# Half the FFN's columns at a time, most of the last group's V kept on chip, and early gradient steps staged in halves

## The chip, the cores and the metric

The kernel runs on one core of a Trainium2 chip. The metric is the device time of one execution in microseconds. A profile of one execution is read beside it.

## What is computed

The reference is a small transformer block for a single token, forward and backward (`jax.vjp`). All tensors are bf16.

```python
def _A_ref(x, k_cache, v_cache, wq, wo):      # D = 448, 16 heads of Dh = 256 over 8 groups
    W = min(4096, max(256, Sk // 4))          # Sk = 32768, so the window is W = 4096
    q = (x @ wq)...
    k = repeat(k_cache[:, :, Sk - W:, :], 2); v = repeat(v_cache[:, :, Sk - W:, :], 2)
    p = softmax(q . k * Dh ** -0.5); o = p . v
    return o.reshape(...) @ wo

def _B_ref(x, w_gate, w_up, w_down):          # F = 1792
    return ((x @ w_gate) * (x @ w_up)) @ w_down

h  = x + _A_ref(layernorm(x), k_cache, v_cache, wq, wo)
h2 = h + _B_ref(layernorm(h), w_gate, w_up, w_down)
# outputs: h2, and the gradients of x, k_cache, v_cache, wq, wo, w_gate, w_up, w_down
```

The gradients of the two caches have the caches' full size, 8 x 32768 x 256 each. They are zero outside the last 4096 positions of each group, and these zeros have to be written as well: 16 regions of 14.68 MB, 235 MB in all.

## The kernel before

**Layout.** Most data lives in `BIG`, one SBUF tile of 128 partitions. It is cut into nine slots of 8192 bf16 columns (`SLOT`, 32 positions of 256), and a tail behind them. A slot holds one group's K or V window: partition p has 32 consecutive positions, 16 KB in one piece. V of group g lies in slot g; K moves through slots 3 to 8 (`K_SLOT`); V of group 7 takes slot 7, after K of group 6.

**Three queues of DMA.** SP issues the fills (`FILL`): each writes one region of zeros from 16 rows of the tile `zeros`, in rows of 8192 (`ZW`) or 14336 columns (`NW`). `next_fills(n)` issues the next n of the list `regions`, and `deal_fill` at the end deals the last region to the DMA engines in uneven parts. POOL (`IO`) issues all loads of windows and weights (`io_load`, in order), the stores of the weight gradients and of `out_2`; `deal_some` sends a few fills there. ACT issues the stores of `out_3`. The scheduler of the framework keeps each engine's order; `in_order` adds an order without a wait. DMAs of SP and ACT take eight completion counters in turn, and a DMA that takes a counter again waits until the one that had it before has landed.

**Forward.** For each group, `moments(g)` (L405) forms the weighted sums over K and V, and issues the next group's scores and softmax. In the last group it also issues the load of wo's first 9 blocks (L435).

**Middle.** After the groups, wo (32 blocks of 448 columns), w_gate, w_up and pieces of w_down are loaded into slot 7, slot 8 and the tail (`A0`, `WU0`, `WG0`, `WD0`, L442 to L446), over V and K of group 7. Fourteen blocks of wo that lie where w_up goes are copied to PSUM first (`park`, L513), since they are needed again. Then come: the product with wo (`ao`, L524), layernorm, the products with all columns of w_gate and w_up (L538), w_down in four pieces (`CH`, `load_wd`, `down_grad` L542, `y` L566), the broadcast of the two gradient rows over the partitions (L578 to L590, into `bc2`), the products with w_gate and w_up (L593), the layernorm's backward pass, and the products with wo (L604). Both rows stay in `bc2` as sources for `out_6` and `out_7`.

**Backward loop.** For each group s = 0 to 7 (L777) 32 outer products are made on PE (`d_ps`, L784), and evicted by ACT and DVE in turn (`evac`, L305 and L307) into a pair of slots (`PAIR`), one for `out_2` and one for `out_3`. At the end of the step both are stored (L814). During a step the products of the next group's V (`dP`) are made, and DVE forms the weight gradients of `during` in pieces (`outer`, L653, with the store at L656). V of group 7, which the weights have overwritten, is loaded again in step 3 (L808). The order in which places become free is what ties a step to the stores of earlier ones:

```python
PAIR = [KS, 0, KS, 0, KS, 0, 5, KS]     # KS = 7
tail = eng.dma_start(out=o[0, g, Sk - W:, :]..., in_=pair[:, w])
```

Of the kernel before, what the change touches and what calls it, by code (L numbers as in the profile page):

```python
# [35 lines left out]
KS = 7  # L36
TAIL = 9 * SLOT
RING = TAIL + 6016
# [5 lines left out]
def kernel(  # L44
# [106 lines left out]
    Vw = [slot_kv(g) for g in range(G - 1)] + [Kw[G - 2]]  # L151
# [253 lines left out]
    def moments(g):  # L405
# [4 lines left out]
        for c in range(T // 2):  # L410
# [31 lines left out]
    A0 = KS * SLOT  # L442
    PARK = range(4, 18)
    WU0 = A0 + PARK[0] * D
    WG0 = A0 + 32 * D
    WD0 = WG0 + NI * HF  # L446
    CH = ((0, 0, 4), (0, 4, NI), (1, 0, 4), (1, 4, NI))
    assert WD0 + 4 * D == RING

    def wo_at(b):  # L450
        return A0 + b * D

# [7 lines left out]
    wg_sb = BIG[:, WG0:WD0]  # L460
    wu_sb = BIG[:, WU0:WU0 + NI * HF]
    wd_sb = BIG[:, WD0:RING].rearrange("p (m n) -> p m n", n=D)
# [4 lines left out]
    bc2 = [BIG[:, o:o + F].rearrange("p (i c) -> p i c", i=2) for o in (WD0, WD0 - F)]  # L467
# [21 lines left out]
    load_wo(9, 32)  # L489
    io_load(wg_sb, flat_rows(B_w_gate))  # L490
# [22 lines left out]
    def park(b):  # L513
        n = (b - PARK[0]) // 2
        w = tps.tile([128, D], u32, tag=f"w{n}", name=f"w{n}")
# [4 lines left out]
    for b in PARK[:-2:2]:  # L520
        park(b)
    ao = tps.tile([1, D], f32, tag="w6", name="ao")
# [4 lines left out]
    hX = const.tile([128, NI], f32)  # L527
    V_.tensor_tensor(out=hX[:], in0=rows_to_half(ao[:])[:], in1=xX[:], op=ALU.add)
    park(PARK[-2])
    io_load(wu_sb[:, 6 * HF:], flat_rows(B_w_up)[:, 6 * HF:])  # L530
    rstd2, xh2, xf2, xx2 = layernorm(hX[:], "ln2")

    gu_ps = ps.tile([128, 2, 2, NI], f32, tag="tmp", bufs=1, name="gu_ps")
    for w, w_sb in ((0, wg_sb), (1, wu_sb)):
        wv = w_sb.rearrange("p (i c) -> p i c", i=NI)
        for m in range(NI):
            for i in range(NI):
                P_.matmul(gu_ps[:, w, :, m], lhsT=wv[:, i, m::NI], rhs=xx2[:, i, :], start=(i == 0), stop=(i == NI - 1))  # L538
# [6 lines left out]
    down_grad(*CH[0])  # L545
    gu = const.tile([128, 2, FC], f32)
    V_.tensor_copy(out=gu[:], in_=gu_ps[:].rearrange("p w s m -> p w (s m)"))

    hh = const.tile([128, FC], f32)
    V_.tensor_tensor(out=hh[:], in0=gu[:, 0, :], in1=gu[:, 1, :], op=ALU.mult)  # L550
    hh_bf = const.tile([128, FC], bf16)
    V_.tensor_copy(out=hh_bf[:], in_=hh[:])

    y = ps.tile([1, D], f32, tag="tmp", bufs=1, name="y")
    hX2 = small.tile([128, NI], f32, tag="hX2", bufs=1)
    V_.tensor_scalar(out=hX2[:], in0=hX[:], scalar1=0.5, scalar2=None, op0=ALU.mult)
    for n, (s, m0, m1) in enumerate(CH):
        if n:
            load_wd(s, m0, m1)
            if n == len(CH) - 1:  # L560
                with tc.issue_after(queued[0].ins):
                    deal_some()
            down_grad(s, m0, m1)
        for m in range(m0, m1):
            c = NI * s + m
            P_.matmul(y[:], lhsT=hh_bf[:, c:c + 1], rhs=wd_sb[:, m - m0, :], start=(c == 0), stop=False, skip_group_check=True)  # L566
# [5 lines left out]
    dgu = const.tile([128, 2, FC], bf16)  # L572
    for w in range(2):
        V_.tensor_tensor(out=dgu[:, w, 0:FC], in0=d_hh[:], in1=gu[:, 1 - w, :], op=ALU.mult)

# [4 lines left out]

    P2 = const.tile([128, 2, NI], f32)
    for w, w_sb, ev in ((0, wg_sb, evac), (1, wu_sb, on_act)):
        for h in range(4):
            r = small.tile([2, HF // 4], bf16, tag="R", name="r")
            t = ps.tile([2, NI, 32], f32, tag="tmp", bufs=1, name="t")
            to_rows(r[:].rearrange("s (j m) -> s m j", m=NI), t[:], [dgu[:, w, m::NI] for m in range(NI)], 32 * h, ev)
            for i2 in range(2):
                bc = ps.tile([128, HF // 4], f32, tag="tmp", bufs=1, name="bc")
                P_.matmul(bc[:], lhsT=Par[:, i2:i2 + 128], rhs=r[:], start=True, stop=True)
                ev(bc2[w][:, i2, h * HF // 4:(h + 1) * HF // 4], bc[:])  # L590
        wv = w_sb.rearrange("p (i c) -> p i c", i=NI)
        for i in reversed(range(NI)):
            V_.tensor_tensor_reduce(out=wv[:, i, :], in0=wv[:, i, :], in1=bc2[w][:, i % 2, :], scale=1.0, scalar=0.0,  # L593
                                    op0=ALU.mult, op1=ALU.add, accum_out=P2[:, w, i:i + 1])
# [8 lines left out]
    for b in range(32):  # L603
        V_.tensor_tensor_reduce(out=wg_sb[:, 0:D], in0=parked.get(b, wo_b(b)), in1=dh_bc[:], scale=1.0, scalar=0.0,  # L604
                                op0=ALU.mult, op1=ALU.add, accum_out=doW[:, b:b + 1])
# [7 lines left out]
    od = small.tile([128, 32], f32, tag="ex", bufs=1)  # L613
# [24 lines left out]
    for b1 in range(0, 16, 4):  # L638
        r = wg_sb[0:2, b1 * 128:b1 * 128 + 512]
# [27 lines left out]
    def wq_product(w, i2, n):  # L667
        V_.tensor_tensor_reduce(out=slot(4)[:, SLOT - HQ:SLOT], in0=w, in1=dq_bc[:, i2, :], scale=1.0, scalar=0.0,  # L668
                                op0=ALU.mult, op1=ALU.add, accum_out=Pq[:, n:n + 1])

    def dxn():
        for h in range(2):
            wq_product(odd[:, h * HQ:(h + 1) * HQ], 0, NI + h)
            yield
# [4 lines left out]
    def dx_out():  # L679
# [12 lines left out]
        dx = slot(4)[0:1, SLOT - D:SLOT]  # L692
# [10 lines left out]
    def o67_job(buf, w, i0, i1):  # L703
        return outer(buf, (o6, o7)[w][:, i0:i1, :], i0, i1, lambda i: bc2[w][:, i % 2, :], xf2, HF)

    def o8_job(buf, b):
# [12 lines left out]
    begin = {3: 4, 5: 8, 6: 8}  # L719
    for job in (o67_job(half(KS + 1, 1), 1, 0, 4), o67_job(half(KS, 1), 1, 4, 7)):  # L720
        for _ in job:
            pass
# [22 lines left out]
    def factors(s):  # L745
        R_ps = ps.tile([128, 2 * Dh], f32, tag="tmp", bufs=1)
        for k, (E, rr) in enumerate(((Ed, do_rows), (Eq, q_rows))):
            ex = small.tile([H, 32, 4], bf16, tag="ex")
# [21 lines left out]

    for q in range(8):
# [5 lines left out]
    for s, g in enumerate(SEQ):  # L777
        R = Rb[:, s % 2, :]
        pair = BIG[:, PAIR[s] * SLOT:(PAIR[s] + 2) * SLOT].rearrange("p (w t d) -> p w t d", w=2, d=Dh)
        work = (None for job in during.get(s, ()) for _ in job)  # L780
        for t in range(T):
# [3 lines left out]
                      start=True, stop=True)  # L785
            if stored is None:
                evac(pair[:, :, t, :], d_ps[:])
            else:
                with tc.issue_after(stored.ins):
                    evac(pair[:, :, t, :], d_ps[:])  # L790
# [3 lines left out]
            if s + 1 < G:  # L794
# [18 lines left out]
        for w, o, eng in ((0, out_3, S_), (1, out_2, IO)):  # L813
            tail = eng.dma_start(out=o[0, g, Sk - W:, :].rearrange("(p t) d -> p t d", t=T), in_=pair[:, w])  # L814
            if eng is S_:
                in_order(tail, filled[0])
                stored = tail
# [36 lines left out]
```

## Time and profile before

| What | Value |
|---|---|
| median of 3 runs | 776.44 us (776.29 to 776.56) |
| the profiled execution: its time, its span | 776.47 us, 774.7 us |
| busy: PE, weight loads, DVE, ACT, POOL | 61%, 34%, 49%, 25%, 4% |
| moved | 330.09 MB: 48.33 read, 280.59 written |
| DMA packets | 19233 |
| first and last DMA of the w_down pieces issued | 269.8 and 333.9 us |
| last stores of the backward loop issued | 702.7 and 703.1 us |

The page cuts the span into 40 slices of 19.4 us and gives the share of busy time in each. Its line for the DMA is the mean over 16 DMA engines. The chain of work that ended last goes back from the last instruction to what released each step. Views by stretch give the busy time of each engine between two points of the span.

### The profile page before, as it was taken

The page shows a single profiled execution, that of the slowest core. Times are in us where ns is not written, and L with a number is a line of the kernel's source. Part 1 is how long each engine was busy: PE and PEld are TensorE (multiplying, and loading weights), DVE is VectorE, ACT ScalarE, POOL GpSimd, SP SyncE. Part 2 cuts the span into 40 slices and gives each one's busy share as a digit, 9 for nine tenths or more (in the row PEclk, how much of TensorE's full clock was granted, in tenths as well). Part 3 has the DMA queues.
Part 4 walks back from the last instruction along what each step waited for, and adds up shares of the span by engine and source line. Part 5 has one row for each costly group of instructions (what it writes and reads, how often), then busy time and mean ns, then how long its engine had stood idle before and what let it go on. Part 6 is the DMA issues. An engine that isn't in the chain of part 4 may idle for free. (4 is left out here: it accounts for less than half of the span.)

```text
span 774.7 us, 10961 instructions
## 1 busy us (share of the span) xinstructions
PE 471.5 (61%) x4427; PEld 263.5 (34%) x4472; DVE 377.3 (49%) x1141; ACT 190.5 (25%) x306; POOL 32.5 (4%) x70
## 2 busy tenths in 40 slices
PE   3889999999996323023315899895786865352000
PEld 2755665556553113011213534332232322120000
DVE  4166566655664112025576465764565545982000
ACT  0422443334220000003102444342242432121000
POOL 3000000000000000010001000000000000000000
PEclk9999999999998665555555555555555555555555
DMA  9999999999999999999999999999999999999998
GB/s 360 429 428 427 428 428 428 427 426 429 428 428 428 430 431 439 427 435 432 429 433 428 429 432 427 435 431 428 430 430 434 430 434 427 432 428 434 433 430 343
DMA packets 19233, 330.09 MB, mean 426 GB/s; under 512 B 1570, under 2 KB 1578, under 8 KB 2847
## 3 DMA queue, kind: packets, MB, share of 16 engines
q1 hardware_dynamic: 10953, 233.91, 70.4%
q0 software_dynamic: 6992, 78.24, 23.9%
q10 hardware_dynamic: 1238, 17.24, 5.2%
q8 instruction: 35, 0.57, 0.3%
q14 instruction: 15, 0.12, 0.0%
HBM read 48.33 MB, written 280.59 MB: 425 GB/s over the span
## 5 line engine op out<-in xcount | busy, mean ns | idle before, releaser
L415 DVE TENSOR_SCALAR BIG<-BIG,pf 128x256 bf16<-128x256 bf16 x512 | 114.7, 282 | 58.8 <-PE MT L419 26.4
L419 PE MATMUL MT<-BIG 128*128 128x512 bf16 x467 | 139.3, 400 | 5.1 <-DMA BIG<-in_A_v_cache_dram 4.3
L784 PE MATMUL d_ps<-BIG 32*128 32x512 bf16 x256 | 118.1, 602 | 39.8 <-DVE BIG L307 17.6
L305 ACT CAST BIG<-d_ps 128x512 bf16<-128x512 f32 x156 | 88.0, 589 | 136.9 <-PE d_ps L784 105.5
L360 PE MATMUL tr<-ident_bf,BIG 128*128 128x128 bf16 x1024 | 119.0, 268 | 4.0 <-DMA BIG<-in_A_k_cache_dram 3.0
L360 PEld LDWEIGHTS <-BIG 128*128 128x128 bf16 x1024 | 79.9, 119 | 40.0 <-issue 35.2
L311 ACT COPY BIG<-tr 128x1024 bf16<-128x1024 bf16 x64 | 64.6, 1012 | 108.9 <-PE tr L360 104.8
L307 DVE CAST BIG<-d_ps 128x512 bf16<-128x512 f32 x100 | 68.5, 687 | 26.2 <-PE d_ps L784 15.6
L422 PEld LDWEIGHTS <-BIG 128*128 128x128 bf16 x512 | 44.8, 99 | 52.0 <-issue 11.7
L307 DVE COPY BIG<-tr 128x1024 bf16<-128x1024 bf16 x60 | 41.4, 690 | 38.7 <-PE tr L360 38.7
L365 PEld LDWEIGHTS <-BIG 128*128 128x128 bf16 x1024 | 38.1, 103 | 62.3 <-DVE BIG L307 42.4
L422 PE MATMUL acc<-pT_all,BIG 128*128 128x2 bf16 x512 | 45.2, 165 | 9.1 <-DVE kbar L439 6.1
L419 PEld LDWEIGHTS <-BIG 128*128 128x128 bf16 x512 | 39.6, 100 | 22.7 <-issue 9.2
L425 PE MATMUL acc<-pT_all,BIG 128*128 128x2 bf16 x512 | 44.2, 164 | 0.0
L784 PEld LDWEIGHTS <-BIG 32*128 32x128 bf16 x256 | 21.2, 113 | 58.8 <-issue 34.9
L365 PE MATMUL dp<-doT,BIG 128*128 128x2 bf16 x512 | 24.3, 169 | 18.6 <-DVE BIG L307 17.5
L542 DVE CUSTOM_DVE_ANT_0 dh_bc<-BIG,dh_bc 128x448 bf16<-128x448 bf16 x14 | 8.7, 624 | 50.9 <-DMA BIG<-in_B_w_down_dram 50.7
L425 PEld LDWEIGHTS <-BIG 128*128 128x128 bf16 x512 | 30.0, 96 | 0.9
L566 PE MATMUL y<-BIG,hh_bf 128*1 128x448 bf16 x14 | 5.9, 565 | 35.9 <-DMA BIG<-in_B_w_down_dram 35.2
L365 PE MATMUL sT<-qT,BIG 128*128 128x2 bf16 x512 | 22.6, 165 | 1.1 <-ACT BIG L311 1.0
L244 PE MATMUL t<-one,xe 1*128 1x1 f32 x42 | 10.8, 323 | 13.1 <-DVE xe L243 13.1
L763 DVE TENSOR_TENSOR BIG<-r_ps,mrow 96x1024 bf16<-96x1024 bf16 (+2 forms) x15 | 18.3, 1223 | 0.8 <-PE r_ps L768 0.4
(192 smaller groups left out, 349.6 us busy)
## 6 DMA issues: line engine op xcount, KB each, us to landing
out_dram<-zeros SPq DMA_DIRECT2D x14, 14336.0 KB, 154.8
out_dram<-BIG POOLq DMA_DIRECT2D x9, 2048.0 KB, 39.3
BIG<-in_A_v_cache_dram POOLq DMA_DIRECT2D x8, 2048.0 KB, 25.8
out_dram<-BIG ACTq DMA_DIRECT2D x8, 2048.0 KB, 22.9
BIG<-in_A_k_cache_dram POOLq DMA_DIRECT2D x6, 2048.0 KB, 43.7
out_dram<-zeros SPq DMA_DIRECT2D x1, 11264.0 KB
out_dram<-zeros SPq DMA_DIRECT2D x1, 7680.0 KB, 61.5
out_dram<-zeros POOLq DMA_DIRECT2D x1, 4224.0 KB, 43.2
```

Of the source, the lines that this page charges most:

```text
L244: P_.matmul(t[:, i:i + 1], lhsT=c, rhs=one[0:1, 0:1], start=True, stop=True)
L305: S_.copy(out=out, in_=in_)
L307: last_copy[0] = V_.tensor_copy(out=out, in_=in_)
L311: S_.copy(out=out, in_=in_)
L360: P_.transpose(tr[:, i, dh, :], x_at(g, 4 * q + i)[:, dh * 128:(dh + 1) * 128], ident_bf[:])
L365: P_.matmul(out_ps[:, 4 * q + i, :], lhsT=xt[:, i, dh, :], rhs=vecT[:, 4 * g + dh:4 * g + dh + 3:2], start=(dh == 0), stop=(dh == 1))
L415: V_.tensor_scalar(out=pk[:, i, h, :], in0=K[:, t, :], scalar1=pf[:, t, h:h + 1], scalar2=None, op0=ALU.mult)
L419: P_.matmul(MT[hf][:], lhsT=v_at(g, t)[:, hf * 128:(hf + 1) * 128], rhs=pk[:, i, :, :].rearrange("p h d -> p (h d)"), start=(t == 0), stop ...
L422: P_.matmul(acc[:, 2 * hf:2 * hf + 2], lhsT=v_at(g, t)[:, hf * 128:(hf + 1) * 128], rhs=pT_all[:, g, t, :], start=(t == 0 and hf == 0), st ...
L425: mm = P_.matmul(acc[:, 4 + dk:7 + dk:2], lhsT=K[:, t, dk * 128:(dk + 1) * 128], rhs=pT_all[:, g, t, :], start=False, stop=(t == T - 1), s ...
L763: V_.tensor_tensor(out=rows[p0:p1], in0=r_ps[p0:p1, :].unsqueeze(1).to_broadcast([p1 - p0, 8, 128]), in1=mrow[p0:p1, :].unsqueeze(2).to_br ...
L784: mm = P_.matmul(d_ps[:].rearrange("p w d -> p (w d)"), lhsT=rows[32 * k:32 * k + 32, a, :], rhs=R[32 * k:32 * k + 32, :], start=True, sto ...
```

## The change

- w_gate and w_up are loaded and used in two halves of 896 columns (`load_wgu`), into the place of wo's first 14 blocks (now in slot 8), which are all copied to PSUM first. A half of w_gate is loaded by ACT in two DMAs, a half of w_up by POOL in two; a row is 1792 B. Gate and up rows are interleaved over partitions, so that one product of DVE covers both.
- wo, gate and up now lie in slot 8 and the tail. In slot 7 only the first 8 positions of V of group 7 are overwritten (`side`: pieces of w_down, the broadcast rows, scratch). These 8 are loaded again, ahead of the loop; the other 24 stay.
- wo comes in three pieces (9, 5 and 18 blocks). `y` is formed as columns (`yc`, `ycol`) and turned at the end.
- The rows for `out_6` and `out_7` are made a second time in the loop (`o67_job`).
- Steps 0 to 2 stage and store their pairs in two halves of 16 positions (`HALVES`), the others in slots two apart (`PAIR`). `out_8` moves from step 6 to ahead of the loop, `out_6` and `out_7` into steps 3 and 4, `out_5` to steps 5 and 6, `out_4` to steps 5 and 6.
- Of the fills, six, one and four are issued in the middle's places, not eleven at the start; fills 5 and 6 have rows of 8192 columns.

```diff
-KS = 7
+KS = 8
+KEPT = 14
+GONE = 8
...
-            f = NW if i >= 5 else ZW
+            f = NW if i >= 7 else ZW
...
-        next_fills(11)
+        next_fills(6)
...
-    Vw = [slot_kv(g) for g in range(G - 1)] + [Kw[G - 2]]
+    Vw = [slot_kv(g) for g in range(G)]
...
+            if c == 13 and g == G - 1:
+                load_wo(9, KEPT)
...
+    wgu_sb = BIG[:, wo_at(0):wo_at(KEPT)].rearrange("p (i c) -> p i c", i=NI)
+    side = BIG[:, (G - 1) * SLOT:(G - 1) * SLOT + GONE * Dh]
+    wd_sb = side[:, 0:4 * D].rearrange("p (m n) -> p m n", n=D)
+    bch = side[:, 0:F].rearrange("p (i c) -> p i c", i=2)
+
+    def load_wgu(h):
+
+        for w, src in ((0, B_w_gate), (1, B_w_up)):
+            rows = src.rearrange("(p r) c -> p r c", r=NI)
+            for e in range(2):
+                i0 = (w + e) % 2
+                n = len(range(i0, NI, 2))
+                d0 = (NI * e + i0 - w) // 2
+                out, in_ = wgu_sb[e::2, i0::2, :], rows[:, d0:d0 + n, h * HF:(h + 1) * HF]
+                if w:
+                    io_load(out, in_)
+                else:
+                    in_order(S_.dma_start(out=out, in_=in_), filled[0])
...
-    load_wo(9, 32)
-    io_load(wg_sb, flat_rows(B_w_gate))
+    load_wo(KEPT, 32)
...
-    io_load(wu_sb[:, 0:6 * HF], flat_rows(B_w_up)[:, 0:6 * HF])
+    load_wgu(0)
+    next_fills(1)
...
+    for f in range(2):
+        half = slice(NI * f, NI * f + NI)
+        if f:
+            load_wgu(1)
+            load_wd(*CH[2])
+            next_fills(4)
+        gu_ps = ps.tile([128, 2, NI], f32, tag="tmp", bufs=1, name="gu_ps")
+        for m in range(NI):
+            for i in range(NI):
+                P_.matmul(gu_ps[:, :, m], lhsT=wgu_sb[:, i, m::NI], rhs=xx2[:, i, :], start=(i == 0), stop=(i == NI - 1))
...
+            for m in range(m0, m1):
+                c = NI * s + m
+                for k in range(4):
+                    P_.matmul(yc[:, k:k + 1], lhsT=wd_sb[:, m - m0, 112 * k:112 * k + 112], rhs=hh_bf[:, c:c + 1],
+                              start=(m == 0 and k == 0), stop=(m == NI - 1), skip_group_check=True)
...
+        for h in range(4):
+            r = small.tile([2, HF // 4], bf16, tag="R", name="r")[:]
+            two_rows([dgu[:, :, NI * f + m] for m in range(NI)], h, r)
+            for i2 in range(2):
+                two_bc(bch, r, i2, h, evac)
+        for i in range(NI):
+            V_.tensor_tensor_reduce(out=wgu_sb[:, i, :], in0=wgu_sb[:, i, :], in1=bch[:, i % 2, :], scale=1.0, scalar=0.0,
+                                    op0=ALU.mult, op1=ALU.add, accum_out=P2[:, f, i:i + 1])
...
     load_odd(IO)
+    IO.dma_start(out=Vw[G - 1][:, 0:GONE, :], in_=A_v_cache[0, G - 1, Sk - W:, :].rearrange("(p t) d -> p t d", t=T)[:, 0:GONE, :])
...
-    PAIR = [KS, 0, KS, 0, KS, 0, 5, KS]
+    HALVES = {0: (0, 8), 1: (1, 0), 2: (2, 8)}
+    PAIR = {3: 1, 4: 2, 5: 3, 6: 4, 7: 5}
     during = {
-        2: [o67_job(slot(2), 0, 0, 7)],
-        3: [o5_job(slot(2), 0)],
-        4: [o5_job(slot(4), 16)],
-        5: [o4_job(slot(2), 0, 4), o4_job(slot(4), 4, 7)],
-        6: [o8_job(half(2, 0), 0), o8_job(half(2, 1), 7), dxn()],
+        3: [o67_job(slot(0), 0)],
+        4: [o67_job(slot(8), 1)],
+        5: [o5_job(slot(1), 0), o4_job(slot(0), 4, 7)],
+        6: [o4_job(slot(2), 0, 4), o5_job(slot(8), 16), dxn()],
         7: [dx_out()],
     }
...
+    def store(g, t0, t1, part):
+        for w, o, eng in ((1, out_2, IO), (0, out_3, S_)):
+            tail = eng.dma_start(out=o[0, g, Sk - W:, :].rearrange("(p t) d -> p t d", t=T)[:, t0:t1, :], in_=part[:, w])
+        in_order(tail, filled[0])
+        return tail
...
+        if s in HALVES:
+            parts = [slot(k).rearrange("p (w t d) -> p w t d", w=2, d=Dh) for k in HALVES[s]]
+        else:
+            parts = [BIG[:, PAIR[s] * SLOT:(PAIR[s] + 4) * SLOT].rearrange("p (w u t d) -> p w u t d", w=2, u=2, d=Dh)[:, :, 0]]
+        n = T // len(parts)
...
-                if t == 26 and s == 3:
-                    Vw[G - 1] = slot_kv(3)
-                    IO.dma_start(out=Vw[G - 1], in_=A_v_cache[0, G - 1, Sk - W:, :].rearrange("(p t) d -> p t d", t=T))
+            if t == n - 1 < T - 1:
+                stored = store(g, 0, n, parts[0])
```

More of the change, by code (lines that the diff above doesn't have):

```diff
@@ L441 @@
     wo_v = A_wo.rearrange("(p b) n -> p b n", p=128)
[L442 to L446, printed above, removed]
     CH = ((0, 0, 4), (0, 4, NI), (1, 0, 4), (1, 4, NI))
-    assert WD0 + 4 * D == RING
     def wo_at(b):
-        return A0 + b * D
+        return KS * SLOT + b * D
     def wo_b(b):
@@ L458, in load_wo @@
         io_load(BIG[:, o:o + (b1 - b0) * D].rearrange("p (b n) -> p b n", n=D), wo_v[:, b0:b1, :])
-    wg_sb = BIG[:, WG0:WD0]
-    wu_sb = BIG[:, WU0:WU0 + NI * HF]
-    wd_sb = BIG[:, WD0:RING].rearrange("p (m n) -> p m n", n=D)
+    assert wo_at(32) == RING and KEPT * D == NI * HF
+    wgu_sb = BIG[:, wo_at(0):wo_at(KEPT)].rearrange("p (i c) -> p i c", i=NI)
[14 more added lines that the diff above has]
+                    in_order(S_.dma_start(out=out, in_=in_), filled[0])
     def load_wd(s, m0, m1):
         io_load(wd_sb[:, 0:m1 - m0, :], wd_rows[:, s].rearrange("j (m n) -> j m n", n=D)[:, m0:m1, :])
-    bc2 = [BIG[:, o:o + F].rearrange("p (i c) -> p i c", i=2) for o in (WD0, WD0 - F)]
     load_V(2)
@@ L511 @@
     parked = {}
-    def park(b):
-        n = (b - PARK[0]) // 2
-        w = tps.tile([128, D], u32, tag=f"w{n}", name=f"w{n}")
+    for b in range(0, KEPT, 2):
+        w = tps.tile([128, D], u32, tag=f"w{b // 2}", name=f"w{b // 2}")
         V_.tensor_copy(out=w[:], in_=BIG[:, wo_at(b):wo_at(b) + 2 * D].bitcast(u32))
@@ L518, in park @@
             parked[b + k] = w[:].bitcast(bf16)[:, k * D:(k + 1) * D]
-    for b in PARK[:-2:2]:
-        park(b)
-    ao = tps.tile([1, D], f32, tag="w6", name="ao")
+    ao = ps.tile([1, D], f32, tag="tmp", bufs=1, name="ao")
     for b in range(32):
         P_.matmul(ao[:], lhsT=oW_bf[:, b:b + 1], rhs=wo_b(b), start=(b == 0), stop=(b == 31))
-    io_load(wu_sb[:, 0:6 * HF], flat_rows(B_w_up)[:, 0:6 * HF])
+    load_wgu(0)
+    next_fills(1)
+    halves = side[0:1, 0:NI * 256].bitcast(f32).rearrange("o (i c) -> o i c", i=NI)
+    for i in range(NI):
+        V_.tensor_copy(out=halves[:, i, :].rearrange("o (m r) -> o m r", r=2), in_=half_cols(ao[:], i))
+    aX = ps.tile([128, NI], f32, tag="tmp", bufs=1, name="aX")
+    for i in range(NI):
+        P_.matmul(aX[:, i:i + 1], lhsT=halves[:, i, :], rhs=one[0:1, 0:1], start=True, stop=True)
+    hX = const.tile([128, NI], f32)
+    V_.tensor_tensor(out=hX[:], in0=aX[:], in1=xX[:], op=ALU.add)
     load_wd(*CH[0])
[L527 to L530, printed above, removed]
     rstd2, xh2, xf2, xx2 = layernorm(hX[:], "ln2")
[L533 to L538, printed above, removed]
     def down_grad(s, m0, m1):
@@ L543, in down_grad, with to_rows, two_rows @@
                                     op0=ALU.mult, op1=ALU.add, accum_out=d_hh[:, c:c + 1])
-    down_grad(*CH[0])
+    def to_rows(dst, t, cols, j0, ev=evac):
+        for j, c in enumerate(cols):
+            P_.matmul(t[:, j, :], lhsT=c, rhs=ident_bf[:, j0:j0 + t.shape[-1]], start=True, stop=True)
+        ev(dst, t)
+    def two_rows(cols, h, r):
+        t = ps.tile([2, NI, 32], f32, tag="tmp", bufs=1, name="t")
+        to_rows(r.rearrange("s (j m) -> s m j", m=NI), t[:], cols, 32 * h, on_act)
@@ L546, with two_bc @@
+    def two_bc(dst, r, i2, h, ev):
+        bc = ps.tile([128, HF // 4], f32, tag="tmp", bufs=1, name="bc")
+        P_.matmul(bc[:], lhsT=Par[:, i2:i2 + 128], rhs=r, start=True, stop=True)
+        ev(dst[:, i2, h * HF // 4:(h + 1) * HF // 4], bc[:])
     gu = const.tile([128, 2, FC], f32)
-    V_.tensor_copy(out=gu[:], in_=gu_ps[:].rearrange("p w s m -> p w (s m)"))
     hh = const.tile([128, FC], f32)
-    V_.tensor_tensor(out=hh[:], in0=gu[:, 0, :], in1=gu[:, 1, :], op=ALU.mult)
     hh_bf = const.tile([128, FC], bf16)
-    V_.tensor_copy(out=hh_bf[:], in_=hh[:])
@@ L554 @@
-    y = ps.tile([1, D], f32, tag="tmp", bufs=1, name="y")
+    dgu = const.tile([128, 2, FC], bf16)
+    P2 = const.tile([128, 2, NI], f32)
+    ycol = const.tile([112, 4], f32)
     hX2 = small.tile([128, NI], f32, tag="hX2", bufs=1)
     V_.tensor_scalar(out=hX2[:], in0=hX[:], scalar1=0.5, scalar2=None, op0=ALU.mult)
[L557 to L566, printed above, removed]
+    for f in range(2):
[6 more added lines that the diff above has]
+        for m in range(NI):
+            for i in range(NI):
+                P_.matmul(gu_ps[:, :, m], lhsT=wgu_sb[:, i, m::NI], rhs=xx2[:, i, :], start=(i == 0), stop=(i == NI - 1))
+        V_.tensor_copy(out=gu[:, :, half], in_=gu_ps[:])
+        V_.tensor_tensor(out=hh[:, half], in0=gu[:, 0, half], in1=gu[:, 1, half], op=ALU.mult)
+        ready = V_.tensor_copy(out=hh_bf[:, half], in_=hh[:, half])
+        yc = ps.tile([112, 4], f32, tag="tmp", bufs=1, name="yc")
+        for s, m0, m1 in CH[2 * f:2 * f + 2]:
+            if m0:
+                load_wd(s, m0, m1)
+                if f:
+                    with tc.issue_after(queued[0].ins):
+                        deal_some()
+            with tc.issue_after(ready.ins):
+                down_grad(s, m0, m1)
+            for m in range(m0, m1):
[3 more added lines that the diff above has]
+                              start=(m == 0 and k == 0), stop=(m == NI - 1), skip_group_check=True)
+        if f == 0:
+            V_.tensor_copy(out=ycol[:], in_=yc[:])
+        else:
+            V_.tensor_tensor(out=ycol[:], in0=ycol[:], in1=yc[:], op=ALU.add)
+        for w in range(2):
+            V_.tensor_tensor(out=dgu[:, w, half], in0=d_hh[:, half], in1=gu[:, 1 - w, half], op=ALU.mult)
+        for h in range(4):
[3 more added lines that the diff above has]
+                two_bc(bch, r, i2, h, evac)
+        for i in range(NI):
+            V_.tensor_tensor_reduce(out=wgu_sb[:, i, :], in0=wgu_sb[:, i, :], in1=bch[:, i % 2, :], scale=1.0, scalar=0.0,
+                                    op0=ALU.mult, op1=ALU.add, accum_out=P2[:, f, i:i + 1])
@@ L567 @@
+    y = ps.tile([1, D], f32, tag="tmp", bufs=1, name="y")
+    for k in range(4):
+        P_.matmul(y[:, 112 * k:112 * k + 112], lhsT=ycol[:, k:k + 1], rhs=ident_f[0:112, 0:112], start=(k == 0), stop=False, skip_group_check=True)
     half_to_row(y[:], hX2[:], False, first=False)
@@ L570 @@
     in_order(S_.dma_start(out=out_0.rearrange("a b d -> (a b) d"), in_=h2), filled[0])
-    dgu = const.tile([128, 2, FC], bf16)
-    for w in range(2):
-        V_.tensor_tensor(out=dgu[:, w, 0:FC], in0=d_hh[:], in1=gu[:, 1 - w, :], op=ALU.mult)
-    def to_rows(dst, t, cols, j0, ev=evac):
-        for j, c in enumerate(cols):
-            P_.matmul(t[:, j, :], lhsT=c, rhs=ident_bf[:, j0:j0 + t.shape[-1]], start=True, stop=True)
-        ev(dst, t)
[L581 to L594, printed above, removed]
     dhn = const.tile([128, NI], f32)
@@ L603 @@
     for b in range(32):
[L604 removed]
+        V_.tensor_tensor_reduce(out=side[:, 1536:1536 + D], in0=parked.get(b, wo_b(b)), in1=dh_bc[:], scale=1.0, scalar=0.0,
                                 op0=ALU.mult, op1=ALU.add, accum_out=doW[:, b:b + 1])
@@ L612 @@
     V_.tensor_copy(out=doT[:], in_=doT_f[:])
-    od = small.tile([128, 32], f32, tag="ex", bufs=1)
+    od = small.tile([128, 32], f32, tag="R", bufs=1)
     V_.tensor_tensor(out=od[:], in0=doT_f[:], in1=oT_f[:], op=ALU.mult)
@@ L665, with wq_product @@
     Pq = const.tile([128, NI + 2], f32)
-    def wq_product(w, i2, n):
-        V_.tensor_tensor_reduce(out=slot(4)[:, SLOT - HQ:SLOT], in0=w, in1=dq_bc[:, i2, :], scale=1.0, scalar=0.0,
+    def wq_product(w, i2, n, junk=odd[:, 0:HQ]):
+        V_.tensor_tensor_reduce(out=junk, in0=w, in1=dq_bc[:, i2, :], scale=1.0, scalar=0.0,
                                 op0=ALU.mult, op1=ALU.add, accum_out=Pq[:, n:n + 1])
@@ L701, in o5_job, with o67_job @@
         return outer(buf, o5[:, b:b + 16, :], b, b + 16, lambda n: dh_bc[:], oW, D)
-    def o67_job(buf, w, i0, i1):
-        return outer(buf, (o6, o7)[w][:, i0:i1, :], i0, i1, lambda i: bc2[w][:, i % 2, :], xf2, HF)
+    bc2 = BIG[:, TAIL + 4096:TAIL + 4096 + F].rearrange("p (i c) -> p i c", i=2)
+    def o67_job(buf, w):
+        for h in range(4):
+            r = BIG[0:2, TAIL + 4096 + F:TAIL + 4096 + F + HF // 4]
+            two_rows([dgu[:, w, m::NI] for m in range(NI)], h, r)
+            yield
+            for i2 in range(2):
+                two_bc(bc2, r, i2, h, V_.tensor_copy)
+                yield
+        yield from outer(buf, (o6, o7)[w], 0, NI, lambda i: bc2[:, i % 2, :], xf2, HF)
     def o8_job(buf, b):
@@ L747, in factors @@
         for k, (E, rr) in enumerate(((Ed, do_rows), (Eq, q_rows))):
-            ex = small.tile([H, 32, 4], bf16, tag="ex")
+            ex = small.tile([H, 32, 4], bf16, tag="R")
             V_.tensor_copy(out=ex[:], in_=E[:, SEQ[s], :].unsqueeze(1).to_broadcast([H, 32, 4]))
@@ L812 @@
             pass
[L813 to L817, printed above, removed]
+        stored = store(g, T - n, T, parts[-1])
         if s % 2 == 0 and regions:
```

21 lines of the change are left out of this document (11 added, 10 removed).

## The prediction

> **What bounds the kernel now.** I read the page's slices and queues first, then busy time by stretch, then the chain and the instructions that came last.
>
> ```profile
> DMA  9999999999999999999999999999999999999998
> GB/s 360 429 428 427 428 428 428 427 426 429 428 428 428 430 431 439 427 435 432 429 433 428 429 432 427 435 431 428 430 430 434 430 434 427 432 428 434 433 430 343
> DMA packets 19233, 330.09 MB, mean 426 GB/s; under 512 B 1570, under 2 KB 1578, under 8 KB 2847
> q1 hardware_dynamic: 10953, 233.91, 70.4%
> q0 software_dynamic: 6992, 78.24, 23.9%
> q10 hardware_dynamic: 1238, 17.24, 5.2%
> ```
>
> The 16 DMA engines are busy from end to end and move 427 to 439 GB/s in every slice but the first and last. q1 is SP's queue (the fills of zeros), q0 POOL's, q10 ACT's; their shares add up to 99.5%. So the time is the bytes and packets of these engines, as long as one queue always holds work.
>
> ```profile
> 437.00:520.00 83.00, 75.19 (x493) 33.54 (x494) 52.58 (x89) 35.56 (x63) 2.52 (x5) 0.50 1.00 430
> 703.00:715.00 12.00, 0.00 (x0) 0.00 (x0) 0.00 (x0) 0.00 (x0) 0.56 (x1) 0.50 1.00 428
> 715.00:740.00 25.00, 0.00 (x0) 0.00 (x0) 0.00 (x0) 0.00 (x0) 0.00 (x0) 0.50 1.01 433
> 740.00:775.00 35.00, 0.00 (x0) 0.00 (x0) 0.00 (x0) 0.00 (x0) 0.00 (x0) 0.50 0.88 379
> ```
>
> Columns: stretch, length, busy us of PE, its weight loads, DVE, ACT, POOL, then clock, DMA share, GB/s. From 703 on nothing computes, and the DMA engines go on for 72 us at full rate.
>
> ```profile
> 519.63 36.12 DMA out_dram<-BIG
> 605.96 41.05 DMA out_dram<-BIG
> ```
>
> ```profile
> 702.67 0.34 ACTq L814 DMA_DIRECT2D out_dram<-BIG  x1
> 703.14 0.56 POOL L814 DMA_DIRECT2D out_dram<-BIG  x1 [6.27 <-issue]
> 710.23 13.68 SPq L89 DMA_DIRECT2D out_dram<-zeros  x3
> ```
>
> Two entries of the chain are waits of the backward loop for stores that must leave a place in BIG: 77 us in sum, and they cost nothing, since the fills use the engines meanwhile. The last stores are issued at 703. By the packet records, the last packet on q10 ends about 48 us before the last of q1, on q0 about 35 us. So compute has slack, and DMA has none.
>
> **The price of a packet**, from the same records (medians): 896 B 41 ns, 2408 B 98, 4096 B 159, 5376 B 206, 8192 B 309, 12544 B 469, 16384 B 611, 28672 B 1062. That is size / 27.2 per ns plus about 8 ns. On one engine the next record starts 4 ns before the last ends, so 4 to 8 ns of a packet are overhead. With two queues busy the engines' time splits 10.0 to 6.1 for 28672 B against 16384 B packets, which is 1062 to 611: one packet from each in turn.
>
> **The change, as load on the DMA engines** (records x ns / 16):
> - V of the last group: 128 packets of 16384 B become 128 of 4096 B: 128 x (611 - 159) / 16 = -3.62 us. This is the only large term. The copies in the built programs add up to 329.39 and 327.81 MB, 1.57 less, so the saving is really there.
> - Gate: 128 packets of 12544 B (3.75 us) become 896 rows of 1792 B on ACT's queue. No record has this size and queue; between 896 B and 2408 B it is 74 ns: 4.14 us, +0.39. At most it is the 2408 B packet's 98 ns (+1.7), at least the line without overhead, 66 (-0.05). I take 74, since both neighbours lie on the line.
> - Up: POOL's queue now groups 1792 B rows by three into 5376 B packets (206 ns). Nine such and one row per engine and half: 3.86 us against 3.78, +0.08.
> - Stores of steps 0 to 2 in halves: 6 x (256 x 309 - 128 x 611) / 16 = +0.34.
> - Fills 5 and 6 with 8192 columns, not 14336: 2 x (896 x 611 - 512 x 1062) / 16 = +0.46.
> - wo in three pieces, out_7 in one: +0.06 and -0.07.
> - 100 DMAs in place of 89, 16 closing records of 9 ns each: +0.10. Some 300 more instructions: one code record of 16 KB (933 ns): +0.06.
>
> Sum -2.20. The overlap of 4 ns on 2,600 more packets gives back 0.65: -2.85. The bounds are -3.6 (all overhead hidden) and -0.9 (rows at 98 ns, no overlap). I take -2.75. The sum belongs to the profiled execution, 776.47 with a span of 774.7, 0.03 off the median: 773.7.
>
> [...]
>
> **The change, as work on the chain** (free while the fills last). Forward part: same instructions. FFN: before, 269.3 (first up load issued) to 383. Gate and up of half 0 can be issued once ao has read wo blocks 0 to 13, before the rest of wo has landed. A gate half is 28 rows per engine, each taking its turn with a fill packet: 28 x (74 + 611) + 9 x 206 ns = 21 us (34 with 28672 B fills; fills 5 and 6 cover 279 to 357 in the trace before, so I take 21). Per half follow the gate and up products (49 pairs, about 7), two w_down pieces (the second 11 us from issue to landing, as before), four turns of rows and broadcast (3.05 each) and 7 products (1.09 each): about 62. Two halves from 262 on end at about 390, 7 us later than now. Behind it the 14 out_8 products (0.33 each), moved ahead of the loop with their two DMAs on POOL, and the V piece, whose DMA stands on POOL ahead of step 0's stores, which come 25 us later anyhow: 5 us. The loop starts 10 to 15 us later.
>
> Then a new wait. SP's and ACT's DMAs share eight completion counters in turn, and in the built program ACT's store of the first half of step 2 waits until fill 10 has landed, that of the second half until fill 11; before, steps 3 and 4 wait for those. Fill 11 ends when SP has moved 179.8 MB and the rest 61.5 (loads 43.1, dealt fills 4.6, out_8 1.6, stores 11.6, code 0.6). Before, 227.5 MB were moved at 531.5, so 241.3 at 531.5 + 13.8 / 0.430 = 564, and fill 10 lands near 525. Steps run 26.9 us each (stores at 464.4, 491.2), so the halves of step 2 would be ready near 518 and 540: ACT holds them, and behind them in its order the next evictions; PE stops once the four d2 buffers are full. Step 3 starts near 564, against 520 now. This takes the place of the 36 us wait. Because it is anchored to a fill, a loop start up to 40 us later moves nothing.
>
> From there: steps 3 and 4 have out_6 and out_7 (8 broadcast copies at 0.39, 7 products at 0.44 on DVE, 4 row copies on ACT), step 5 out_5 and part of out_4 (16 x 0.33 + 3 x 0.75); these mostly fit beside the evictions, 29, 29 and 31. Steps 6 and 7 are DVE's: 29 us of products (4 x 0.75, 16 x 0.33, 9 x 2.28), 34 of its own, 65 in all; before, DVE was busy 47 of the last 55. End near 564 + 154 = 718, against 703. The stores that free places are two steps back, and q0 gets 16 to 24 packets per engine and step, each with a fill packet's turn: 27 to 43 us, so another 10 us of waiting is possible: 728. The 4.2 MB of step 7 need 10 us, and landing 2 to 3. So the chain costs nothing until its last stores are issued at about 759.
>
> **Rivals.**
> - *Small packets and the slowest engine eat part.* Rows at 98 ns, no overlap: 775.5. By the records the engines end between 767.7 and 774.7, mean 772.9; what is added need not fall evenly, and one code record on the last engine is 0.9. For: 1792 B rows on q10 are not in the trace. Against: all sizes lie on one line. Time 775.3, within 0.2%.
> - *The backward chain becomes the end.* Place: the stores of steps 3 to 7. Steps 3 to 7 take 183.5 us now with their waits (519.6 to 703.1); from 564 that gives 747.5, still covered. It decides from 759, that is with 195 us or more, and then each us costs one; with 200 the end is near 779. For: fill 11 holds step 2, and out_4, two of out_5, out_6 and out_7 now all queue in steps 3 to 6. Against: halves and places freed in turn take two steps of distance.
> - *Each added DMA costs its latency.* A w_down piece of 336 KB takes 10.9 us to land; its 4 packets per engine, each behind a fill packet, need 4 x (206 + 1062) = 5.1. If the other 5.8 were exposed on each of the 11, 64 us: 838. Against: the engines have no gap to show for the 89 there are. [...]
>
> That the bytes are not saved can't be, as the built copies show.
>
> **How the numbers follow.** What a measurement can tell from no change is about 0.2%, 1.55 us: 774.9 and 778.0. The forecast, 773.7, has 0.70, all of it faster; small packets and the slowest engine 0.15, same; the chain 0.11 and latency 0.04, slower. The forecast with its bounds and the spread of the engines' ends reaches from 772.5 to 774.9; to leave out no more than 2 in 10 the range takes in the first rival and the start of the second, up to 777.0.
>
> **What would show it.** Right: about 328.5 MB moved, the slices still 9 throughout, last stores issued between 710 and 745, ACT idle in step 2 ahead of its stores at about 525 and 564, gate halves landing some 21 us after issue, the last packets being SP's. Wrong: slices under 9 between 700 and 760 (the chain), gate packets far off 74 ns, or engine ends spread by over 8 us.

## The result, and the profile after

The changed kernel takes 775.14 us (774.89 to 775.43, 17 runs), the kernel before 776.43 (17 runs): ratio 0.9984, 95% interval 0.9976 to 0.9991. So it is faster, by 1.3 us where 2.75 were forecast. The profiled execution of the changed kernel takes 774.92 us with a span of 773.1.

The page, slices and queues (queue, kind, packets, MB, share of 16 engines):

```profile
DMA  9999999999999999999999999999999999999997
GB/s 360 429 428 430 426 426 429 429 428 426 424 427 429 431 429 429 430 436 430 434 425 435 432 426 427 431 430 432 427 428 436 427 428 431 438 425 433 426 433 316
DMA packets 21859, 328.54 MB, mean 425 GB/s; under 512 B 1746, under 2 KB 2682, under 8 KB 4191
q1 hardware_dynamic: 11721, 233.91, 70.6%
q0 software_dynamic: 7456, 75.06, 23.0%
q10 hardware_dynamic: 2630, 18.85, 5.8%
```

1.55 MB less are moved, in 2,626 packets more, and the engines are still full throughout. Only the last slice is emptier than before: 316 GB/s against 343. The busy time by stretch shows that compute now ends at about 738 and no longer at 703:

```profile
703.00:715.00 12.00, 1.90 (x4) 0.37 (x4) 12.00 (x14) 0.00 (x0) 0.00 (x0) 0.50 1.02 438
715.00:740.00 25.00, 16.55 (x61) 7.10 (x61) 16.13 (x33) 9.08 (x16) 1.59 (x3) 0.50 1.00 426
740.00:774.00 34.00, 0.00 (x0) 0.00 (x0) 0.00 (x0) 0.00 (x0) 0.00 (x0) 0.50 0.83 356
```

The instructions of the program's end tell where the rest of the gain went. First the kernel before, then the changed one, from the view of that source line (engine, operation, count, duration in ns min/median/max, start of the first and the last in us):

```profile
L849 POOLq DRAIN  x3: 40/102/37709, 703.1 to 774.4; - x3
L849 SPq DRAIN  x3: 7/7/13, 773.9 to 774.2; - x3
```

```profile
L891 POOLq DRAIN  x3: 45/93/34482, 737.9 to 772.9; - x3
L891 SPq DRAIN  x3: 7/7/7, 770.7 to 772.6; - x3
```

These drains stand at the program's end. SP comes to the first of them behind its waits for DMAs in that line (49.4 us in sum before, 86.6 after) and 0.9 and 0.6 us after the last DMA record: at 773.9 before, at 770.7 after, 3.2 us earlier. I take it as the point where SP has seen all DMAs land. POOL's first drain stands behind its last store: before, from 703.1 for 37.7 us, so until 740.8, long done; after, from 737.9 for 34.5 us, until 772.4. The span ends 0.7 us behind that. By the packet records, the last record of q1 ends at 772.9 before and at 770.2 after, 2.8 us earlier, and the last of q0 now ends 0.8 us before that of q1 (35 us before). So the engines gave about what was forecast, and half of it was lost again at the end, where POOL became the last.

### The profile page after: what moved, and what is told of

Read it like the earlier page. It is cut to its first block, busy times and chain, and to the rows that moved or that the text cites. A ratio compares the mean times of both kernels' runs of the same rounds, so it can differ in the third digit from the quotient of the medians.

```text
span 773.1 us, 11276 instructions
## 1 busy us (share of the span) xinstructions
PE 487.5 (63%) x4549; PEld 273.1 (35%) x4594; DVE 385.3 (50%) x1166; ACT 199.1 (26%) x312; POOL 36.1 (5%) x74
## 4 chain that ended last, share of the span: by engine, by line
PE 52%; DMA 17%; DVE 16%; issue 4%; ACT 4%; another core or an unknown queue 2%; ACTq 0%; POOLq 0%; DVEq 0%
PE MT L421 13%; PE tr L362 11%; PE d_ps L830 11%; DMA BIG<-in_B_w_gate_dram 9%; DVE BIG L309 3%; DMA BIG<-in_B_w_down_dram 3%; DVE BIG L630 3%; DVE Mt L695 3%; PE sT L367 3%; DMA BIG<-in_A_wo_dram 3%; DMA BIG<-in_A_k_cache_dram 2%; PE acc L424 2%; PE dp L367 2%; DVE BIG L612 2%; DMA BIG<-in_A_v_cache_dram 2%
## 5 line engine op out<-in xcount | busy, mean ns | idle before, releaser
L830 PE MATMUL d_ps<-BIG 32*128 32x512 bf16 x256 | 123.3, 612 | 36.8 <-DVE BIG L799 17.4
L421 PE MATMUL MT<-BIG 128*128 128x512 bf16 x467 | 141.2, 406 | 2.5 <-DMA BIG<-in_A_v_cache_dram 1.7
L307 ACT CAST BIG<-d_ps 128x512 bf16<-128x512 f32 x156 | 89.9, 594 | 127.3 <-PE d_ps L830 96.4
L362 PEld LDWEIGHTS <-BIG 128*128 128x128 bf16 x1024 | 79.6, 119 | 43.1 <-issue 38.8
L424 PEld LDWEIGHTS <-BIG 128*128 128x128 bf16 x512 | 44.1, 98 | 50.0 <-issue 8.1
L367 PEld LDWEIGHTS <-BIG 128*128 128x128 bf16 x1024 | 38.4, 103 | 50.0 <-DVE BIG L309 20.5
L582 PE MATMUL gu_ps<-xx,BIG 128*128 128x2 bf16 x98 | 5.5, 193 | 75.3 <-DMA BIG<-in_B_w_gate_dram 75.3
L421 PEld LDWEIGHTS <-BIG 128*128 128x128 bf16 x512 | 40.6, 102 | 23.5 <-issue 15.2
L313 ACT CAST r<-t 2x224 bf16<-2x224 f32 x8 | 8.1, 1012 | 122.1 <-PE t L553 122.1
L582 PEld LDWEIGHTS <-BIG 128*128 128x128 bf16 x98 | 5.4, 153 | 76.3 <-issue 76.3
L427 PEld LDWEIGHTS <-BIG 128*128 128x128 bf16 x512 | 30.0, 96 | 0.9
```

Source lines behind the costliest of these rows:

```text
L307: S_.copy(out=out, in_=in_)
L313: S_.copy(out=out, in_=in_)
L362: P_.transpose(tr[:, i, dh, :], x_at(g, 4 * q + i)[:, dh * 128:(dh + 1) * 128], ident_bf[:])
L367: P_.matmul(out_ps[:, 4 * q + i, :], lhsT=xt[:, i, dh, :], rhs=vecT[:, 4 * g + dh:4 * g + dh + 3:2], start=(dh == 0), stop=(dh == 1))
L421: P_.matmul(MT[hf][:], lhsT=v_at(g, t)[:, hf * 128:(hf + 1) * 128], rhs=pk[:, i, :, :].rearrange("p h d -> p (h d)"), start=(t == 0), stop ...
L424: P_.matmul(acc[:, 2 * hf:2 * hf + 2], lhsT=v_at(g, t)[:, hf * 128:(hf + 1) * 128], rhs=pT_all[:, g, t, :], start=(t == 0 and hf == 0), st ...
```

## The experiments

Two theories. **A**: the DMA engines' work fell by what the sum says, and POOL's drain behind the last out_2 store ends the span. **B**: the packets, or the spread of the engines' ends, cost more than forecast, and POOL's end is only near.

**The last store on ACT.**

```diff
-        for w, o, eng in ((1, out_2, IO), (0, out_3, S_)):
+        for w, o, eng in ((1, out_2, IO if g < G - 1 else S_), (0, out_3, S_)):
```

Expected:

> The changed kernel, but the last step's out_2 store is issued by ACT, not by POOL; nothing else moves. Theory A (POOL's end): in the trace after, SP has seen its last DMA at 770.7 (773.9 before), 3.2 us earlier than before, but POOL's drain, which began at 737.9 behind that store, lasts 34.5 us and ends at 772.4; the span of 773.1 is POOL's. Then, without that store on POOL, POOL's drain ends some 10 us earlier, the span follows SP: 770.7 + 0.8 = 771.5, 1.6 us less than after, time near 773.5 (ratio to before 0.9963). Theory B (the packets and the engines' ends cost more than forecast, POOL's end is only near): the same packets are moved, so the time stays at 775.1 within 0.3.

Measured: 773.96 us, ratio 0.9970 (0.9959 to 0.9982). POOL's drain and SP's:

```profile
L891 POOLq DRAIN  x3: 40/93/37911, 728.0 to 772.0; - x3
L891 SPq DRAIN  x3: 7/7/7, 771.5 to 771.8; - x3
```

POOL ends at 765.9, SP at 771.5, the span at 772.3. The same packets, and 1.2 us less than the changed kernel: theory A. It is 0.5 us short of what I expected, because SP's own end came at 771.5 and not 770.7; among the versions that move the same bytes, in the table below, that end lies between 770.7 and 771.5 in all but the last row.

**The bytes alone.** In the kernel before, only 8 of 32 positions are loaded again:

```diff
-                    IO.dma_start(out=Vw[G - 1], in_=A_v_cache[...])
+                    IO.dma_start(out=Vw[G - 1][:, 0:8, :], in_=A_v_cache[...][:, 0:8, :])
```

> The kernel before, but of V of the last group only 8 of 32 positions are loaded again in step 3 (the other 24 hold other data, so that part of the computation is left out). This is the term of the bytes alone: 128 packets of 16384 B become 128 of 4096 B. If the DMA engines' work is the time: -3.6 us, 772.8 (ratio 0.9953), as its last stores are issued at 703 and leave 34 us. If less than 2 us come (774.4 or more), the saved bytes are not worth what the records say, and the forecast failed in its largest term.

Measured: 772.62, ratio 0.9954 (0.9940 to 0.9967), 3.63 us less than its kernel before (776.25). The largest term, -3.62, is what this run gave, in which POOL's drain ends 36.5 us before SP has seen all DMAs land. That -3.62 and -3.63 agree to 0.01 us is chance, as the interval is 1 us to either side.

**w_gate on POOL.**

```diff
-                if w:
-                    io_load(out, in_)
-                else:
-                    in_order(S_.dma_start(out=out, in_=in_), filled[0])
+                io_load(out, in_)
```

> The changed kernel, but the halves of w_gate are loaded by POOL in its order, ahead of w_up, not by ACT. In the trace after, ACT issues the first half at 281.3, behind the square root of the layernorm in its own order, and gate and up products wait for it until 310; half 2 is issued at 344.7. On POOL the first half is issued near 269, the rows are grouped by three, so 9.3 turns and not 28: landed near 285, half 2 some 12 us sooner too, and the backward loop starts 30 to 37 us earlier. DMA work: about -0.2 us. In the built program ACT's store of the second half of step 2 still waits for fill 11. Theory A with that anchor: ACT waits there from about 525 until 570, the last stores are issued near 738 as before, and the time stays at 775.1 (to 774.6). Rival: the FFN's length sets the last stores; then they come 30 us earlier, near 708, and the time is 773.3.

Measured: 775.23, ratio 0.9985 (0.9976 to 0.9994): no change against the changed kernel. The issues of ACT's stores for step 0's first half and for step 2's two halves, in the changed kernel:

```profile
495.01 0.38 ACTq L809 DMA_DIRECT2D out_dram<-BIG  x1
547.93 0.34 ACTq L809 DMA_DIRECT2D out_dram<-BIG  x1
570.45 0.34 ACTq L809 DMA_DIRECT2D out_dram<-BIG  x1
```

and with w_gate on POOL:

```profile
460.80 0.38 ACTq L806 DMA_DIRECT2D out_dram<-BIG  x1
533.70 0.34 ACTq L806 DMA_DIRECT2D out_dram<-BIG  x1
572.92 0.34 ACTq L806 DMA_DIRECT2D out_dram<-BIG  x1
```

The loop starts 34 us earlier, and step 2 ends 2.5 us later. The last store is issued at 740.5. The anchor to fill 11 holds, as forecast, and it was not the FFN's length that set the last store.

**w_gate and out_0 on POOL.** The diff above, and `IO.dma_start` for out_0.

> As the run with w_gate on POOL, and out_0 is stored by POOL too. With one DMA less on ACT, the second half of step 2 takes the counter of fill 10 and not of fill 11 (the first half that of fill 9). Theory A: ACT's wait ends at about 525 and not 570, the last stores are issued 30 to 40 us earlier, between 698 and 712, POOL's drain ends long before SP's, the span follows SP: time 773.2 (ratio 0.996). Theory B: 775.

Measured: 773.80, ratio 0.9971 (0.9960 to 0.9982). Step 2's halves are stored at 532.6 and 545.3, the last store is issued at 716.5, POOL's drain ends at 760.6, and SP's end at 771.2 sets the span of 772.0. Theory A again, though the last store came 4 us later than expected. ACT's copy of dh waited 31.1 us for the store of out_0; the next run has that wait alone.

**out_0 alone on POOL.**

> The changed kernel with out_0 alone moved to POOL; w_gate stays on ACT. ACT's store of the second half of step 2 then takes the counter of fill 10 and not of fill 11. Nothing else of the chain changes, so in step 2 ACT's wait of 9 us (570.45 against POOL's 561.10) should be gone and the last stores come near 729, not 738. Theory A: POOL's drain then ends before SP's, and the time is 773.9 (ratio 0.9970). If the wait on the counter is of no account: 775.1.

Measured: 775.86, ratio 0.9995 (0.9986 to 1.0004): 0.7 us slower than the changed kernel, against my expectation; the lowest of its runs, 775.59, is above the highest of the changed kernel's, 775.43. The counter's wait is gone (577.5 on ACT, 578.0 on POOL). But the list of waits has a new one:

```profile
ACT dh_bc L627 <- DMA out_dram<-dh_bc: 31.3, 1, 31.3
```

out_0 is stored out of the first row of `dh_bc`, and the next writer of `dh_bc` waits until it has landed. On POOL's queue, issued behind the dealt fills, it took 30.9 us to land. The loop started 17 us later, the last store came at 747.7, POOL's drain ended at 773.0. So this run does not tell what the counter's wait alone is worth.

**The price of a packet.** The kernel before, with rows of 8192 columns in all fills (`f = ZW`):

> The kernel before with rows of 8192 columns in all fills: 10 fills more with 896 and not 512 packets per DMA, 240 packets more on each engine and no other bytes. It measures the overhead of a packet. With 4 to 5 ns (records less their overlap): +1.1 us, 777.5 (ratio 1.0014). With the 8 to 9 ns of the records alone: +2.0 us, 778.4 (ratio 1.0027). Two kernels that end with the DMA engines (last out_2 store on ACT, and w_gate with out_0 on POOL) came out at -2.3 and -2.4 us where the sum said -2.75, and -2.2 without the overlap; this run tells which of the two holds.

Measured: 777.38 against 776.29, ratio 1.0013 (1.0004 to 1.0022). 3,840 packets more cost 1.09 us, that is 1090 / 240 = 4.5 ns each on its engine. The interval allows 1.3 to 7 ns, so the records less their overlap (4 to 5) hold, and the 8 to 9 of the records alone are out.

**The chain later by known amounts.** The seven products of wq a second (and a third) time in step 6:

> The changed kernel with the 7 products of dxn over wq made a second time in step 6 (the same results; 16 us of DVE work more, no DMA). Last stores at about 754. The forecast says the chain costs nothing until 759; then 775.1 to 775.4. By theory A POOL's end already sets the time and moves with its last store, but less than one for one, since the fills run out sooner and the store then has the engines for itself: issue 754 + about 2 until its first packet + 9.8 for the 4.2 MB of the step + some 2.5 until POOL's drain ends + 0.7 = 769 to 773 if alone, so not before the 773.1 of now, and the engines still have all the fills to do: time between 775.1 and 776. One for one would be 791.

> The same with 14 such products, 32 us: last stores at about 770. Past the point: 770 + 2 + 9.8 + 2.5 + 0.7 = 785 span, 787 time (ratio 1.0135); the fills end before, near 767, and the engines stand idle for some us. If the chain still cost nothing, 775.

Measured: 775.50, ratio 0.9990 (0.9981 to 0.9999), and 778.77, ratio 1.0027 (1.0016 to 1.0038). The last out_2 store was issued at 753.5 and at 762.9. 16 us of delay cost 0.4 us; 9 us more cost 3.3. The second run (776.96 to 779.08) came out 8 us under what I expected, since its last out_2 store came at 762.9 and not 770: 32 us of products moved it by only 25. From its issue to POOL's drain end, 776.2, it took 13.3 us; my terms for that were 14.3, but they were made up otherwise. By the packet records the fills ended at 760.5, and the engines had nothing to do until ACT's store of out_3 began at 763.3. POOL's packets began only at 768.2, 5.4 us after the issue and when ACT's were nearly done (I took 2, an estimate that no trace shows for POOL: in the changed kernel POOL's first load, issued at 1.3, had its first packet at 5.4). The two stores, 4.2 MB, took 10 us, and POOL's drain ended 3.0 us behind them.

**Fills 5 and 6 as before, with w_gate and out_0 on POOL.**

> A version from what the runs show: w_gate and out_0 on POOL, and fills 5 and 6 with 14336 columns as before (768 packets fewer, -0.2 to -0.4 us). w_gate's and w_up's turns now stand against 28672 B packets: the loop starts some 12 us later than with 8192, which the places behind it hide as long as the last stores come before about 737. Time 773.4 (ratio 0.9965).

Measured: 776.11, ratio 0.9997 (0.9989 to 1.0006). A miss: the loop started 28 us later than with 8192 columns (step 0's first half stored at 507.5, not 479.6), the last store came at 744.2, and POOL's drain at 772.9 set the end. Fewer packets, but the small rows of the weights took their turns against 28672 B packets: the last rows of the second half came at 371.9, at 346.6 with 8192 columns. The median is also 0.6 us above the profiled execution (775.55); why is not shown.

**Both cures.** w_gate on POOL, the last out_2 store on ACT:

> Both cures together: w_gate on POOL, and the last out_2 store on ACT. The chain stays tied to fill 11 (last stores near 740, as with w_gate on POOL alone), POOL's drain ends some 6 us before SP's. Theory A: the DMA engines set the end as in the two runs at -2.3 and -2.4 us, so no more is to be had: 773.8 (0.9970). If the early loop start had a worth of its own: 773.3 or less.

Measured: 773.67, ratio 0.9965 (0.9951 to 0.9978), against 776.37 for the kernel before. This is the best version. Against w_gate on POOL alone, which differs in the last out_2 store only, it is 1.6 us less: the same test of theory A a second time. The drains with w_gate on POOL alone, then with both:

```profile
L888 POOLq DRAIN  x3: 45/93/32329, 740.5 to 773.3; - x3
L888 SPq DRAIN  x3: 7/7/7, 771.2 to 773.1; - x3
```

```profile
L888 POOLq DRAIN  x3: 40/102/36182, 729.0 to 771.5; - x3
L888 SPq DRAIN  x3: 7/7/13, 771.0 to 771.3; - x3
```

All profiled ends side by side (us; the median in the last column is of the timed runs):

| Kernel | last POOL DMA issued | POOL's drain ends | SP has seen all | span | median |
|---|---|---|---|---|---|
| 8192 columns in all fills | 696.0 | 717.3 | 775.0 | 775.8 | 777.38 |
| short reload | 696.3 | 733.5 | 770.0 | 770.9 | 772.62 |
| before | 703.1 | 740.8 | 773.9 | 774.7 | 776.43 |
| w_gate and out_0 on POOL | 716.5 | 760.6 | 771.2 | 772.0 | 773.80 |
| last store on ACT | 728.0 | 765.9 | 771.5 | 772.3 | 773.96 |
| both cures | 729.1 | 765.2 | 771.0 | 771.9 | 773.67 |
| changed | 737.9 | 772.4 | 770.7 | 773.1 | 775.14 |
| w_gate on POOL | 740.5 | 772.8 | 771.2 | 773.6 | 775.23 |
| fills 5, 6 as before | 744.2 | 772.9 | 770.8 | 773.7 | 776.11 |
| out_0 on POOL | 747.7 | 773.0 | 770.9 | 773.8 | 775.86 |
| chain 16 us later | 753.5 | 773.0 | 771.0 | 773.8 | 775.50 |
| chain 32 us later | 765.8 | 776.2 | 774.1 | 777.0 | 778.77 |

In every row the span is 0.7 to 0.9 us behind the later of the two ends. The first three rows are the kernel before and its two variants. The medians between 775.1 and 776.1 do not follow the order of the last store, and that scatter is not explained.

## Why the prediction was right, and where it was wrong

- **The work of the DMA engines: right.** The -3.62 us of the bytes measured -3.63. There are 2,449 more data packets in the records, and in the run with 8192 columns in all fills one cost 4.5 ns beside its bytes (1.3 to 7). The gate rows, of which the trace before had none on this queue, took 74 ns. For the whole sum, -2.75, there are three measures: the last record of q1 ends 2.8 us earlier in the changed kernel; with the last store on ACT, which moves the same packets, the time is 2.3 us less; with both cures it is 2.7 less, but there w_gate's rows also go in fewer packets, worth an estimated 0.2 to 0.35 (by the records). The intervals of the last two, about 1 us to either side, hold the sum.
- **"So the chain costs nothing until its last stores are issued at about 759": the step that failed.** It asked only whether the engines would run out of work, and its 10 us for the last 4.2 MB give the last stores the engines to themselves. In the changed kernel, from the last issue at 737.9 on, q0 still had 4.2 MB to move (2.1 of the last store, the rest of earlier DMAs) and q10 2.1, beside 6.7 of fills on q1, and the last record of q0 came 31.5 us after that issue. POOL's drain ended 2.8 us after the last record of its queue in the kernel before and 3.0 in the changed one, while SP had seen all land 0.9 and 0.6 us after the last record of all. So the backlog on q0, which ended nearly together with the fills (769.4 and 770.2 in the changed kernel), made POOL's drain the last by 1.6 to 2.1 us in the changed kernel and four variants, with last stores at 738 to 753, before compute was late enough to leave the engines idle. That is the missing half of the gain: without it the time was 1.2 us less in one pair of versions and 1.6 in the other. Last stores at 738 to 753 cost 0 to 1 us more than the changed kernel's, in no clear order. Past that there is one run: 9 us more cost 3.3, and there the fills had ended at 760.5. So a first knee was missed, and the second, forecast at 759, was about right as far as one run shows.
- **The FFN, forecast 7 us later than before: wrong in size.** The copy of dh into `dh_bc` comes at 433.9, and at 390.4 before: 43 us. Two reasons, both in the load of w_gate; with that load on POOL the copy came at 399.7. ACT issues it in its own order, behind the square root of the second layernorm, and not once wo's blocks are read:

```profile
280.91 0.26 ACT L276 ACTIVATE rstd<-t,eps_t 128x1 f32<-128x1 f32 x1 [30.97 <-PE t L262]
281.28 2.37 ACTq L476 DMA_DIRECT2D BIG<-in_B_w_gate_dram  x2
```

```profile
PE gu_ps L582 <- DMA BIG<-in_B_w_gate_dram: 75.3, 2, 48.3
```

  The first half was 19 us later than the 262 I took, and landed by 307.7: 26 us, forecast 21. The second was issued at 344.7 and landed by 385.8: 41 us. The turns themselves were priced rightly: from the first row to the last it took 21 us, and 36 in the second half; 4 us before the first row and 1 us behind the last were not in the sum. I had 34 in the text for turns against 28672 B fills and chose 21, as fills 5 and 6 lasted to 357 before; in the trace after, fill 6 was done on most engines by about 348, as the second half's rows began. The run with fills 5 and 6 as before shows the same price once more.
- **The wait on the fill: right in kind, smaller in size.** The first half of step 2 came at 547.9, forecast 525, when the step was ready and not for a fill; the second waited for fill 11:

```profile
570.88 1.56 ACT L307 CAST BIG<-d_ps 128x512 bf16<-128x512 f32 x3 [12.21 <-DMA out_dram<-zeros]
```

  Forecast 564, found 570.5. That the loop's start moves nothing as long as the fill is later was right: a start 34 us earlier moved the last store by 2.6 us, in the wrong direction. But of the 40 us of room the late start left only 12: with the loop 17 us later still (out_0 alone on POOL) the last store came 10 us later. From there to the last store it took 167 us, where 154 to 164 were forecast.
- **The rivals.** By size, 1.3 us is the case that I called "same" and gave 0.15; but its mechanism, dearer packets and the slowest engine, is not what happened: rows took 74 ns and not 98, and q1's last record was 2.8 us earlier. That the time still lies within the range to 777.0 is in part luck: the forecast with its own bounds ended at 774.9, and the range was widened for this rival and the next. The chain as the end, 0.11, had the right place and the wrong price. Latency of the added DMAs: nothing of it, the version with both cures has all 11 and is 2.7 us faster than the kernel before. In the changed kernel four of them are POOL's and seven ACT's, by their closing records.
- **Slips in the working, none of which moves the forecast.** The ninth slice before moved 426 GB/s, not 427 or more. Products of 28.8 us and 34 of DVE's own make 63, not 65. Twenty-four turns of 611 and 1062 ns make 40 us, not 43. Counted from the span's start the last DMA record ends at 772.9, so the ends of the engines, given up to 774.7, are 1.8 us too late.

## What to carry to other kernels

Where the transfers set the time, count bytes and packets, and look apart from that at which queue's end the program itself waits for last: here POOL's queue held a small last part of the work (4.2 MB at its last issue) while the engines were still full, and its drain ended 1.7 us after SP had seen all DMAs land. Give the last transfers to a queue whose end the program sees soonest (here ACT's, not POOL's, for 1.2 and 1.6 us), and look in the built program which earlier DMA a store has to wait for because of a shared counter (here fill 11, until 570.5). A load on an engine that also computes starts when that engine's order comes to it, not when its place is free (w_gate on ACT at 281.3, where I took 262), and a store of a buffer that is written again soon must not stand behind a long queue (here the next writer waited 31.3 us).

## What the runs showed of the hardware that was not expected

- POOL's drain at the end lasted until 2.7 to 3.2 us after the last record of its queue, in all twelve kernels (2.8 before, 3.0 in the changed one); SP had seen all DMAs land 0.6 to 1.0 us after the last record of any queue (0.9 and 0.6). What POOL's drain does in that time is not shown here.
- In the changed kernel, rows of 1792 B went one by one on ACT's queue (896 packets of 74 ns) and by three on POOL's (5376 B, 206 ns). In the first half's load 448 rows stand beside 495 fill packets of 16384 B in the same 21 us, in the second's beside 477, nearly all of 28672 B, in 36 us: about one fill packet to a row.
